# Seven unread 16-byte-row loads on the scalar engine's DMA queue, ahead of the first softmax of a decode block

## The chip, the cores and the metric

The kernel runs on one NeuronCore of a Trainium2 chip. The metric is the time of one execution on the device in microseconds (us); lower is better. The core has five engines with a queue of instructions each: PE (TensorE: matmuls, its weight loads shown as PEld), DVE (VectorE), ACT (ScalarE), POOL (GpSimd) and SP (SyncE, which here only issues DMAs). A transfer (a DMA) is issued by an instruction in the queue of SP or of ACT and is then carried by 16 DMA engines, which add to a semaphore as their shares land. In the trace SPq and ACTq are the issuing sides.

## What is computed

One decode step of a transformer block with adaptive layer norm, batch 2, one token each, all in float32: a modulation from a condition vector, attention of 32 query heads over the last 4096 positions of a cache with 8 key/value heads, and a feed-forward part.

```python
W = min(4096, max(256, Sk // 4))                      # 4096 of 32768 positions
q = (h @ wq) ...                                      # 32 heads of 128
k, v = k_cache[:, :, Sk - W:], v_cache[:, :, Sk - W:] # 8 heads, each for 4 query heads
p = softmax(q k^T * Dh ** -0.5);  attn = (p v) @ wo
mod = (silu(c) @ w_mod) -> sa, ca, ga, sb, cb, gb
x = x + ga * attn(layernorm(x) * (1 + ca) + sa)
x = x + gb * (silu((layernorm(x) * (1 + cb) + sb) @ w1) @ w2)
```

Nearly all the bytes are read once: 6.3 MB of `w_mod`, 8.4 MB of `wq`, 33.6 MB of keys, 33.6 MB of values, 8.4 MB of `wo`, 7.3 MB of `w1` and `w2`.

## The kernel before

All large inputs stream through one on-chip buffer, `slots` (line 68): a ring of eight slots of 16 KB on each of 128 partitions. `stream` (line 70) hands out slots in turn, and `load_runs` (line 88) and `load_pair` (line 77) issue one large DMA each on SP. In the order of SP's queue they are `w_mod` (three slots), the small `x`, `wq` (four slots), and then keys and values in pairs of slots. One step is one batch entry with two key/value heads; there are `STEPS` = 8 of them. The DMA of the keys of step s is called k0 to k7 here, that of the values v0 to v7, 4 MB each; each wants two free slots. `fetch` (line 349) issues them in the order k0, k1, v0, k2, v1, k3, v2, k4, and so on; `wo`, `w1` and `w2` follow (lines 506, 511, 600).

v0 and k2 go into the four slots that held `wq`, so they may start when the matmuls that make q (line 302) have read those slots. v1 goes into the slots of k0, k3 into those of k1, v2 into those of v0, and so on: a key load waits until DVE has transposed the keys that stood there (`keys`, line 361), and a value load until PE has used the old contents (`weighted`, line 448).

The work of a step: DVE transposes the keys (line 361), PE makes the scores (`scores`, line 374), DVE and PE find the maxima (`maxima`), ACT takes the exponential (`exponentials`: a copy of the bias at line 404, the activation at line 406), DVE and PE turn the weights (`turn`), ACT copies them to `ptb` (line 435), and PE multiplies them with the values (`weighted`, line 448). `place(0)` (line 334) comes ahead of step 0: it lays q out in `qbd` with copies on DVE, POOL and ACT (lines 319 and 329). `inorder` keeps an engine's instructions in the order in which they are written.

The framework gives each DMA one of eight semaphores (DMAHW0 to DMAHW7) to report its landing on. They are given out in turn, in the order in which the program's DMAs stand, over both issuing queues. A DMA that takes a semaphore which an earlier DMA has used waits for that earlier DMA to land before it is issued; the waits stand in the issuing engine's queue, which goes on with nothing behind them until they are met. In the program before, `w_mod` has DMAHW0, the four loads of `c` on ACT have 1 to 4, `x` has 5, `wq` 6, k0 7, k1 0 again, v0 1 again, k2 2, v1 3 and k3 4.

Of the kernel before, what the change touches and what calls it, by code (L numbers as in the profile page):

```python
# [13 lines left out]
P = 128  # L14
# [9 lines left out]
def adaln_block(  # L24
# [19 lines left out]
    nc = tc.nc  # L44
# [16 lines left out]
    def const(shape, name):  # L61
        return consts.tile(shape, F32, name=name)

    def bank(tag, name):
        return (psum1 if tag in "CO" else psum).tile([P, 512], F32, tag=tag, name=name)
# [244 lines left out]
    inorder = tc.keep_in_program_order  # L310

    def place(n):

        qT = once.tile([P, D], F32, tag="wide", name=f"qT{n}").rearrange("p (s j r) -> p s j r", s=4, r=32)
        inorder(nc.vector.transpose(qT.rearrange("p s j r -> p (s j r)"), q_ps[n]))  # L315
        for g in range(G):
            r = slice(32 * g, 32 * g + 32)
            eng = nc.gpsimd if g % 2 else nc.vector
            inorder(eng.tensor_copy(  # L319
                qg[n][r, :, :, :, g], qT[r, :, :, 0:32:16].rearrange("p s j b -> p s b j")  # L320
            ))
        rp = bank("C", f"qr{n}")[:, :P]
        inorder(nc.tensor.matmul(  # L323
            rp, rep4, qg[n].rearrange("p s b j g -> p (s b j g)"), start=True, stop=True
        ))
        for i in range(4):
            r = slice(32 * i, 32 * i + 32)
            cp = nc.scalar.copy if i % 2 else nc.vector.tensor_copy
            inorder(cp(
                qbd[n][r].rearrange("p s b j c -> p (s b j) c")[:, :, 4 * i : 4 * i + 4],  # L330
                rp[r, :].rearrange("p (m g) -> p m g", g=G),
            ))

    place(0)

# [394 lines left out]
```

## Time and profile before

| | |
|---|---|
| time, median of 2 runs | 235.64 us (235.56 to 235.73) |
| span of the profiled execution, first to last instruction | 233.7 us |
| own time of the profiled execution | not recorded beside its span; the timed runs lie 1.9 to 2.0 us above the span |
| bytes read | 97.53 MB, 417 GB/s over the span |
| PE busy | 161.1 us (69%) |
| DVE busy | 115.6 us (49%) |
| ACT busy | 28.5 us (12%) |
| POOL busy | 10.5 us (4%) |

The page of the profile gives busy time by engine, the DMA queues (q1 carries what SP issues, q10 what ACT issues, q8 and q14 instructions), and the chain of work that ended last. The timeline lists instructions with their start and length. The view of DMA issues tells how long after the start of its issue a DMA had fully landed. The view by windows gives for any stretch the mean busy share of the 16 DMA engines and the rate; shares a little above 1 come from counting each packet whole in the stretch in which it starts.

### The profile page before, as it was taken

The page shows a single profiled execution, that of the slowest core. Times are in us where ns is not written, and L with a number is a line of the kernel's source. Part 1 is how long each engine was busy: PE and PEld are TensorE (multiplying, and loading weights), DVE is VectorE, ACT ScalarE, POOL GpSimd, SP SyncE. Part 2 cuts the span into 40 slices and gives each one's busy share as a digit, 9 for nine tenths or more (in the row PEclk, how much of TensorE's full clock was granted, in tenths as well). Part 3 has the DMA queues.
Part 4 walks back from the last instruction along what each step waited for, and adds up shares of the span by engine and source line. Part 5 has one row for each costly group of instructions (what it writes and reads, how often), then busy time and mean ns, then how long its engine had stood idle before and what let it go on. Part 6 is the DMA issues. An engine that isn't in the chain of part 4 may idle for free.

```text
span 233.7 us, 2571 instructions
## 1 busy us (share of the span) xinstructions
PE 161.1 (69%) x1070; PEld 43.3 (19%) x1070; DVE 115.6 (49%) x179; ACT 28.5 (12%) x64; POOL 10.5 (4%) x35
## 2 busy tenths in 40 slices
PE   0004916859577839797598749759759779789684
PEld 0001401201111111211120201202112122324222
DVE  0007240278894758695197089259559540101232
ACT  2000210000311120120210201111020120102020
POOL 2004710000000000000000000000000000000000
PEclk9999985979999977999979999988997997999999
DMA  7998998999999999999999999999999999989991
GB/s 269 446 542 359 404 494 359 446 444 421 415 421 449 446 437 415 426 426 446 449 437 409 418 437 449 449 421 412 426 444 449 443 421 437 463 367 437 424 404 57
DMA packets 3794, 97.68 MB, mean 418 GB/s; under 512 B 432, under 2 KB 456, under 8 KB 968
## 3 DMA queue, kind: packets, MB, share of 16 engines
q1 hardware_dynamic: 3768, 97.53, 97.1%
q8 instruction: 8, 0.13, 0.2%
q14 instruction: 2, 0.02, 0.0%
q10 hardware_dynamic: 16, 0.00, 0.0%
HBM read 97.53 MB, written 0.00 MB: 417 GB/s over the span
## 4 chain that ended last, share of the span: by engine, by line
DMA 60%; issue 18%; DVE 14%; PE 6%; POOL 0%; SPq 0%; POOLq 0%; ACT 0%
DMA slots<-in_A_k_cache_dram 22%; DMA slots<-in_A_wq_dram 15%; DMA slots<-in_A_v_cache_dram 12%; DMA slots<-in_B_w_dram 12%; DVE kT L361 11%; PE o L448 2%; PE q L302 2%; DVE zp L420 1%; PE acc_yw L661 1%; DVE xp L418 1%; PE qr L323 0%; PE acc_y L671 0%; DVE qT L315 0%; POOL qg L319 0%; SPq L109 0%
## 5 line engine op out<-in xcount | busy, mean ns | idle before, releaser
L361 DVE STREAM_TRANSPOSE kT<-slots 128x1024 f32<-128x1024 f32 x64 | 73.7, 1212 | 23.7 <-DMA slots<-in_A_k_cache_dram 23.6
L374 PE MATMUL s<-kT,qbd 128*32 128x512 f32 x256 | 68.6, 693 | 19.1 <-DVE kT L361 18.0
L448 PE MATMUL o<-slots,ptb 128*32 128x512 f32 x256 | 30.8, 624 | 2.1 <-DMA slots<-in_A_v_cache_dram 2.1
L374 PEld LDWEIGHTS s<-kT,qbd 128*32 128x32 f32 x256 | 9.6, 113 | 68.4 <-DVE kT L361 63.4
L269 PE MATMUL m_a<-slots,scT 128*32 128x256 f32 x32 | 4.4, 506 | 20.5 <-DVE scT L261 20.5
L302 PE MATMUL q<-slots,hq_T 128*32 128x512 f32 x64 | 8.3, 680 | 7.0 <-DMA slots<-in_A_wq_dram 7.0
L448 PEld LDWEIGHTS o<-slots,ptb 128*32 128x32 f32 x256 | 8.1, 114 | 17.9 <-issue 17.8
L404 ACT COPY bias<-bp 128x1 f32<-128x1 f32 x8 | 1.3, 159 | 77.0 <-PE bp L402 77.0
L384 DVE TENSOR_REDUCE mx<-s 128x1 f32<-128x512 f32 x8 | 5.5, 691 | 9.6 <-PE s L374 9.6
L565 PE MATMUL junk<-quad,id 128*32 128x512 f32 x22 | 10.2, 595 | 0.0
L420 DVE TENSOR_TENSOR zp<-xp,quarter 128x1024 f32<-128x1024 f32 x8 | 9.8, 1225 | 0.2
L435 ACT ACTIVATE ptb<-pT,odd 128x256 f32<-128x256 f32 x16 | 6.7, 472 | 25.6 <-PE pT L427 25.6
L255 DVE STREAM_TRANSPOSE cT<-xc 128x128 f32<-128x128 f32 x1 | 0.4, 401 | 16.7 <-DMA xc<-in_c_dram 16.7
L427 PE MATMUL pT<-zp,mix 128*32 128x256 f32 x64 | 5.7, 428 | 3.6 <-DVE zp L420 3.5
L458 ACT COPY ob<-o 128x512 f32<-128x512 f32 x8 | 4.7, 585 | 26.1 <-PE o L448 26.1
L272 PE MATMUL m_sp<-slots,scT 128*32 128x512 f32 x32 | 7.4, 738 | 0.0
L386 PE MATMUL mT<-ident,mx 128*1 128x128 f32 x16 | 3.0, 270 | 6.3 <-DVE mx L384 6.3
L315 DVE STREAM_TRANSPOSE qT<-q 128x512 f32<-128x512 f32 x2 | 1.4, 717 | 11.7 <-PE q L302 10.2
L418 DVE STREAM_TRANSPOSE xp<-pr 128x512 f32<-128x512 f32 x8 | 5.5, 686 | 3.4 <-ACT pr L406 3.4
L579 PE MATMUL acc_o<-slots,oTn 128*32 128x512 f32 x56 | 6.2, 593 | 0.7 <-DMA slots<-in_A_wo_dram 0.7
L466 PE MATMUL o_all<-ob,selh 128*64 128x128 f32 x64 | 6.0, 316 | 0.8 <-ACT ob L458 0.8
L550 DVE COPY acc_o_sb<-acc_o 128x256 f32<-128x256 f32 x1 | 0.4, 425 | 12.4 <-ACT acc_o_sb L549 12.4
(140 smaller groups left out, 93.8 us busy)
## 6 DMA issues: line engine op xcount, KB each, us to landing
slots<-in_A_k_cache_dram SPq DMA_DIRECT2D x8, 4096.0 KB, 27.4
slots<-in_A_v_cache_dram SPq DMA_DIRECT2D x8, 4096.0 KB, 27.6
slots<-in_w_mod_dram SPq DMA_DIRECT2D x1, 6144.0 KB, 17.1
slots<-in_A_wo_dram SPq DMA_DIRECT2D x1, 6144.0 KB
slots<-in_B_w_dram SPq DMA_DIRECT2D x1, 2688.0 KB
slots<-in_A_wo_dram SPq DMA_DIRECT2D x1, 2048.0 KB, 29.5
slots<-in_B_w_dram SPq DMA_DIRECT2D x1, 2048.0 KB
slots<-in_B_w_dram SPq DMA_DIRECT2D x1, 896.0 KB
```

The source lines that it names most:

```text
L272: nc.tensor.matmul(m_sp[r, :], scT[:, k, :], cd[:, g], start=(k == 0), stop=(k == 3))
L302: nc.tensor.matmul(q_ps[n][32 * g : 32 * g + 32, :], hq_T[:, k, :], wv[:, n, g], start=(k == 0), stop=(k == 3),)
L361: inorder(nc.vector.transpose(kT[s, j][:, 32 * c : 32 * c + 32, :], kt[s].rearrange("p (n j r) -> p j n r", j=4, r=32)[:, j, 32 * c : 32 * ...
L374: inorder(nc.tensor.matmul(s_ps[s][r : r + 32, :], qbd[h // 4][:, h % 4, b, j, :], kT[s, j][:, 32 * c : 32 * c + 32, e:32:2], start=(j == ...
L418: inorder(nc.vector.transpose(xp, pr[s]))
L420: inorder(nc.vector.tensor_mul(zp, xp[:, None, :, 0:16].to_broadcast([P, 4, 16, 16]), quarter[:, :, None, None].to_broadcast([P, 4, 16, 16 ...
L427: inorder(nc.tensor.matmul(tp[32 * i : 32 * i + 32, :], mix.rearrange("p v e -> p (v e)"), zp.rearrange("p y t x -> p (y t) x")[:, :, 4 * ...
L435: inorder(nc.scalar.activation(ptb[s % 2][:, :, e, :], tp.rearrange("p (w z) -> p w z", z=16), AF.Copy, scale=odd[:, e : e + 1],))
L448: inorder(nc.tensor.matmul(o_ps[s][r : r + 32, :], ptb[s % 2][:, w].rearrange("p e z -> p (e z)"), vt[s].rearrange("p (c w m f d) -> p c f ...
L466: inorder(nc.tensor.matmul(o_all[r : r + 64, :], selh[:, m, lo : lo + 2 * HQ], o_sb[s][:, m * DH : (m + 1) * DH], start=(s == 0 and m < 2) ...
L565: inorder(nc.tensor.matmul(junk[0:32, :], id4, quad.rearrange("p m y -> p (m y)"), start=True, stop=True,))
L579: inorder(nc.tensor.matmul(acc[32 * g : 32 * g + 32, :], oTn[:, q, :], wot[q], start=(q < 4), stop=(q >= 24),))
```

## The change

Three lines after `place(0)`: a small tile `spare`, and seven loads on ACT's queue of the first four elements (16 bytes) of the first 8, 12, 6, 14, 10, 1 and 3 rows of `w2`. Nothing reads `spare`. The output is computed as before.

```diff
     place(0)
+    spare = const([P, 7, 4], "spare")
+    for i, n in enumerate((8, 12, 6, 14, 10, 1, 3)):
+        inorder(nc.scalar.dma_start(spare[:n, i, :], w2[:n, :4]))
```

ACT's queue in the changed program, from the copy of the modulation through the copies of `place(0)` to the exponential of step 0; `spare` is the new tile, `in_B_w_dram` the input `w2`, and the names in brackets are the semaphores an instruction waits for (DMAHW: landings of DMAs, the others: engines):

```order
L286 COPY mod_sp<-m_sp 128x512 [waits PE_49]
L329 COPY qbd_151<-qr_280 32x32x4 [waits DVE_49] x2
L337 DMA spare<-in_B_w_dram 8x4 [waits DMAHW1_49]
L337 DMA spare<-in_B_w_dram 12x4 [waits DMAHW2_49]
L337 DMA spare<-in_B_w_dram 6x4 [waits DMAHW3_49]
L337 DMA spare<-in_B_w_dram 14x4 [waits DMAHW4_49]
L337 DMA spare<-in_B_w_dram 10x4 [waits DMAHW5_49]
L337 DMA spare<-in_B_w_dram 1x4 [waits DMAHW6_49]
L337 DMA spare<-in_B_w_dram 3x4 [waits DMAHW7_49]
L407 COPY bias_336<-bp_334 128x1 [waits PE_49]
L409 ACT_TABLE_LOAD [waits DVE_49]
```

Before, the bias copy (then line 404) followed directly on the copies of line 329. The seven loads stand between them and take the semaphores DMAHW1 to DMAHW7, each waiting for the landing of the DMA that had it: the four loads of `c`, `x`, `wq` and k0.

SP's queue before, the first six loads of keys and values (k0, k1, v0, k2, v1, k3):

```order
L82 DMA slots<-in_A_k_cache_dram 128x1x8192 [waits DMAHW0_49,PE_49]
L82 DMA slots<-in_A_k_cache_dram 128x1x8192 [waits PE_49]
L82 DMA slots<-in_A_v_cache_dram 128x1x8192 [waits DMAHW6_49,DMAHW1_49,PE_49]
L82 DMA slots<-in_A_k_cache_dram 128x1x8192 [waits DMAHW2_49,PE_49]
L82 DMA slots<-in_A_v_cache_dram 128x1x8192 [waits DMAHW7_49,DMAHW3_49,DVE_49]
L82 DMA slots<-in_A_k_cache_dram 128x1x8192 [waits DMAHW4_49,DMAHW0_49,DVE_49]
```

SP's queue in the changed program, the same six loads:

```order
L82 DMA slots<-in_A_k_cache_dram 128x1x8192 [waits DMAHW0_49,PE_49]
L82 DMA slots<-in_A_k_cache_dram 128x1x8192 [waits PE_49]
L82 DMA slots<-in_A_v_cache_dram 128x1x8192 [waits DMAHW6_49,DMAHW0_49,PE_49]
L82 DMA slots<-in_A_k_cache_dram 128x1x8192 [waits DMAHW1_49,PE_49]
L82 DMA slots<-in_A_v_cache_dram 128x1x8192 [waits DMAHW7_49,DMAHW2_49,DVE_49]
L82 DMA slots<-in_A_k_cache_dram 128x1x8192 [waits DMAHW3_49,DVE_49]
```

The loads stand in the same order. The seven new DMAs have moved the turn of the semaphores on: v0 now takes DMAHW0, which k1 has, and waits for it in place of DMAHW1, which a load of `c` had. k2, v1 and k3 wait for the semaphores of the first three new loads in place of those of the loads of `c`, and the wait of k3 for DMAHW0 (k1, whose slots it takes) is no longer there, since SP has met it already for v0. On PE, DVE and POOL the same instructions stand in the same order, with the semaphores of the loads renumbered.

## The prediction

> **What bounds the kernel now.** I read the page first, for the share of the DMA queues and the chain that ended last; then the view by windows, to see whether the DMA engines ever pause; then the timeline of SP and the view of DMA issues, for when each load is issued and lands; and last ACT and DVE at the place of the change. The page:
>
> ```profile
> span 233.7 us, 2571 instructions
> ...
> q1 hardware_dynamic: 3768, 97.53, 97.1%
> q8 instruction: 8, 0.13, 0.2%
> ...
> DMA 60%; issue 18%; DVE 14%; PE 6%; POOL 0%; SPq 0%; POOLq 0%; ACT 0%
> ```
>
> The queue of the large loads alone keeps 16 engines busy for 97.1% of the span, and DMA is the largest part of the last chain. By windows (the last two columns are the busy share of the DMA engines and GB/s):
>
> ```profile
> 0.00:1.70 1.70, 0.00 (x0) 0.00 (x0) 0.27 (x1) 0.00 (x0) 1.09 (x8) 1.00 0.00 0
> 1.70:4.20 2.50, 0.00 (x0) 0.00 (x0) 0.00 (x0) 0.38 (x1) 0.52 (x2) 1.00 0.98 315
> 36.00:56.00 20.00, 15.11 (x90) 3.69 (x90) 9.43 (x12) 0.51 (x2) 0.47 (x2) 0.82 1.01 434
> 56.00:76.00 20.00, 14.36 (x70) 2.80 (x72) 14.53 (x18) 4.00 (x9) 0.00 (x0) 1.00 0.99 429
> ...
> 176.00:196.00 20.00, 16.39 (x110) 4.93 (x112) 10.51 (x15) 2.26 (x6) 0.00 (x0) 0.85 1.00 429
> 196.00:216.00 20.00, 17.78 (x149) 6.60 (x140) 1.66 (x6) 2.24 (x3) 0.00 (x0) 0.98 0.99 424
> 216.00:226.00 10.00, 7.82 (x45) 2.31 (x44) 3.39 (x17) 1.77 (x3) 0.00 (x0) 1.00 0.98 419
> ```
>
> From 1.7 us on the DMA engines do not pause, up to 226. The chain of waits, three pieces of it:
>
> ```profile
> 92.88 22.90 DMA slots<-in_A_k_cache_dram
> ...
> 126.84 27.70 DMA slots<-in_A_k_cache_dram
> ...
> 165.61 27.61 DMA slots<-in_A_v_cache_dram
> ...
> 198.74 27.57 DMA slots<-in_B_w_dram
> 226.30 0.14 issue
> 226.44 1.92 PE acc_yw L661 x16
> ```
>
> k4 lands at 92.88 + 22.90 = 115.78, k6 at 154.54, v7 at 193.22. From k4 to k6 four loads land (v3, k5, v4, k6), from k6 to v7 four more: 38.76 / 4 and 38.68 / 4, so a load of 4096 KB takes 9.68 us, or 433 GB/s, at both places. The end hangs on the same stream: the first large piece of `w2` lands at 226.30 and PE starts on it at once. So the kernel is one unbroken stream of bytes, and 233.7 - 226.3 = 7.4 us of the span are left when that piece is in. There is no later pause in which a delay of the stream could be made good: a pause of the DMA engines in the middle comes out at the end, one for one.
>
> **The seven loads themselves.** Where they stand:
>
> ```profile
> 46.40 0.26 ACT L329 COPY qbd<-qr 32x128 f32<-32x128 f32 x1 [15.43 <-DVE qbd L329]
> 47.01 0.26 ACT L329 COPY qbd<-qr 32x128 f32<-32x128 f32 x1 [0.35 <-DVE qbd L329]
> 60.61 0.16 ACT L404 COPY bias<-bp 128x1 f32<-128x1 f32 x1 [13.35 <-PE bp L402]
> ```
>
> The only loads on ACT before are the four of `c`:
>
> ```profile
> 1.16 2.62 ACTq L105 DMA_DIRECT2D xc<-in_c_dram  x4
> ```
>
> Issuing is 2.62 / 4 = 0.65 us each, so seven take 4.6 us: from 47.27 to 51.9, inside the 13.35 us in which ACT waits for PE. Their own semaphore waits cost nothing there: the last is for k0, which lands one load ahead of k1, and k1 lands at 57.8 (below), so at 48.1. Their 54 rows of 16 bytes are 864 bytes. Packets cost time too, and the nearest row is that of the packets of `c`, which pass beside `w_mod`, in the view of DMA queues from 6 to 17.3 us (packets, MB, share of 16 engines):
>
> ```profile
> q10 hardware_dynamic: 16, 0.00, 0.2%
> ```
>
> 0.2% of 16 engines for 11.3 us is 0.36 us for 16 packets, 0.02 us each. The first engine of the 16 gets at most seven rows and seven semaphore packets, some 0.3 us if all fall on one engine's bulk work. I take 0.1 and keep 0 to 0.4.
>
> **The wait that they move.** This is where I put the cost. In the changed order v0 waits for DMAHW0, held by k1 (the built program asks for a count of 32, 16 for `w_mod` and 16 for k1). When was v0 issued, and when does k1 land?
>
> ```profile
> 0.73 0.38 SPq L93 DMA_DIRECT2D slots<-in_w_mod_dram  x1
> ...
> 29.08 1.84 SPq L82 DMA_DIRECT2D slots<-in_A_k_cache_dram  x2
> 43.97 0.54 SPq L82 DMA_DIRECT2D slots<-in_A_v_cache_dram  x1
> 45.69 0.54 SPq L82 DMA_DIRECT2D slots<-in_A_k_cache_dram  x1
> 57.38 0.53 SPq L82 DMA_DIRECT2D slots<-in_A_v_cache_dram  x1
> ```
>
> The second of the two issues at 29.08, k1, starts at 30.37, and the view of DMA issues for that stretch says:
>
> ```profile
> slots<-in_A_k_cache_dram SPq DMA_DIRECT2D x1, 4096.0 KB, 27.4
> ```
>
> So k1 lands at 30.37 + 27.4 = 57.8. v0 goes from 43.97 to 57.8, and behind it on SP stand k2 (45.69, now 58.4) and v1 (57.38, now about 59). Before, two loads were queued when k1 ended; now none is: the stream runs dry once. k2 also waits for the first new load and v1 for the second. The four of `c` took until DVE could start on them, after 16.7 us of idle time:
>
> ```profile
> L255 DVE STREAM_TRANSPOSE cT<-xc 128x128 f32<-128x128 f32 x1 | 0.4, 401 | 16.7 <-DMA xc<-in_c_dram 16.7
> ```
>
> That is about 4 us each, one after the other, beside the bulk; issued from 47.3 on, the first two land by 52 and 56, before 58. The later ones are wanted by loads that are issued after 70.
>
> What does starting the stream again cost? The nearest row is the one start from nothing, `w_mod`:
>
> ```profile
> slots<-in_w_mod_dram SPq DMA_DIRECT2D x1, 6144.0 KB, 17.1
> ```
>
> At 433 GB/s its 6144 KB take 1.5 x 9.68 = 14.5 us, so the start costs 17.1 - 14.5 = 2.6 us from issue to landing. Issuing a key or value load takes 0.54 in place of 0.38, 0.16 more: 2.7. The Trainium skill, on "SBUF — State Buffer", section "The DMA setup-cost knee", gives every DMA a roughly fixed 2 us beside its bytes; by that the forecast below would be 238.1 in place of 238.8, and this trace's row says 2.6. As bounds: the windows show an empty 0.73 to 1.7, 1.0 us, as the least; the most I keep is 4.0, since a start in mid-program isn't shown.
>
> Who is late, then: v0 lands at 57.8 + 2.7 + 9.7 = 70.2, and PE wants it at 74.86, when the maxima of step 1 are done. k2 lands at 79.9 where DVE took it at 77.15:
>
> ```profile
> 74.86 3.64 PE L448 MATMUL o<-slots,ptb 128*32 128x512 f32 x32
> ...
> 77.15 2.37 DVE L361 STREAM_TRANSPOSE kT<-slots 128x1024 f32<-128x1024 f32 x2 [2.71 <-DMA slots<-in_A_k_cache_dram]
> ```
>
> DVE was waiting for it already, so from here on every step is 2.7 us late, and the stream with it.
>
> One more term. The 16 engines don't end a load together, and the trace tells a landing by the last. q8 fetches code: 8 packets, 0.2% of 16 x 233.7 us, so 0.9 us each, on one engine at a time. In an unbroken stream an engine that is ahead hides such a fetch; after the dry spell all 16 start level, and the next fetch shows at the end, in part or whole: 0 to 0.9, I take 0.4.
>
> The sum: 0.1 + 2.7 + 0.4 = 3.2 us on a span of 233.7, so 236.9; the median of the runs lies 1.94 above the span, so 238.8 us, or 1.4% more than 235.64.
>
> **The rivals.**
> *Nothing happens* (the wait is met in time, or the stream has a reserve). For it: v0 isn't wanted before 74.86. Against it: the DMA share, which has no hole to give back. It gives 235.6 to 236.1. The Trainium skill, on "DMA: Bandwidth & Descriptors", section "Issuing engines are not separate DMA queues", has DMAs from several engines interleave on the same 16 DMA engines, so that only the time to issue differs; by it alone this rival would hold, as it says nothing of a moved wait. The packets of q10 between those of q1 agree with it. 8%.
> *Slower by over 2%: a dearer restart.* The same dry spell with a price that `w_mod` at an idle chip doesn't show, or with code fetches falling on one engine after the engines have been levelled. It decides from 4.72 - 0.5 = 4.2 us on, against 2.7; two fetches on one engine (1.8 in place of 0.4) and a restart of 3 would reach it. It gives 240.4 to 242. For it: the price rests on one row. Against it: nothing in that row looks short. 10%.
> *The softmax is held up.* If ACT's queue were held until all seven had landed, that would be till about 47.3 + 7 x 4 = 75 and not 51.9, and the exponential of step 0 would come 14 us late; v1 and k3 would still be queued behind k2 till 57.8 + 2.7 + 3 x 9.7 = 89.6, so most of it is hidden and the result is that of the forecast or the rival above. It has no chance of its own.
> *Faster.* The uneven row counts delay low engines more than high ones; if that made them pass each other better, the rate would rise. To come out 2% faster, the stream left at 57.8, 226.3 - 57.8 = 168.5 us of it, would have to run 2.8% above the 433 GB/s that both stretches of the chain show, and there is no idle time of the DMA engines after 1.7 us to save. 2%, 230.9 at that point.
>
> **How the numbers follow.** The forecast has 80%, the null rival 8%, the dear restart 10%, faster 2%. The forecast's own range comes from the bounds: 1.0 to 4.0 for the restart, 0 to 0.4 for the packets, 0 to 0.9 for the levelling, which all at their ends would be 236.6 to 240.9; that all lie at one end is unlikely, so I take 237.0 to 240.3, which leaves out the null rival, the dear one and little more. Two per cent, 4.7 us, is about what a measurement of this kernel tells from no change: faster 0.02, within 0.88, slower 0.10.
>
> **What would show it.** SP should issue v0 at about 57.8 with a wait on a DMA, k2 and v1 within 1.5 us behind it, and the windows from 57 to 61 should show DMA shares far below 1, the only ones before the tail. k2's keys should start on DVE near 79.9, and every later load should land 2.7 to 3.6 us later than before. ACT's bias copy should stay at 60.6. If v0 is issued at 44, the step of the moved wait is wrong; if the dry spell is there and the end is not late, the claim that no reserve is left is wrong; if the stream is dry a second time, I have missed a wait.

## The result, and the profile after

The changed kernel takes 239.7 us (239.5 to 239.9, 2 runs) against 235.64: the ratio is 1.0169, with a 95% interval of 1.0139 to 1.0198, so 4.1 us more. The forecast was 238.8 us in a range of 237.0 to 240.3. The profiled execution spans 238.1 us, 4.4 more than before.

From the page after (span, DMA share in 40 slices of 6 us, queues):

```profile
span 238.1 us, 2578 instructions
...
DMA  7998989993999999999999999999999999999991
...
q1 hardware_dynamic: 3768, 97.53, 95.7%
...
q10 hardware_dynamic: 124, 0.01, 0.0%
```

The row of nines has one hole: the tenth slice, 53.6 to 59.5 us, has 3. The bytes are the same, and q10 has 108 packets more: 54 rows and 54 reports to a semaphore. The timeline of SP for the first value and key loads after k1 (start, length):

```profile
58.30 0.54 SPq L82 DMA_DIRECT2D slots<-in_A_v_cache_dram  x1
58.94 0.55 SPq L82 DMA_DIRECT2D slots<-in_A_k_cache_dram  x1
59.59 0.54 SPq L82 DMA_DIRECT2D slots<-in_A_v_cache_dram  x1
72.12 0.54 SPq L82 DMA_DIRECT2D slots<-in_A_k_cache_dram  x1
```

v0, k2 and v1 go out together behind k1's landing, where before they went at 43.97, 45.69 and 57.38. The view of waits on SP between 25 and 75 us names the releaser (total, times, longest):

```profile
SPq L82 <- DMA slots<-in_A_k_cache_dram: 27.8, 1, 27.8
```

The view by windows, the last two columns being DMA share and GB/s:

```profile
57.00:58.00 1.00, 0.96 (x6) 0.14 (x4) 0.80 (x1) 0.00 (x0) 0.00 (x0) 1.00 0.00 0
58.00:59.00 1.00, 0.94 (x4) 0.00 (x0) 0.01 (x1) 0.00 (x0) 0.00 (x0) 1.00 0.00 0
59.00:60.00 1.00, 0.26 (x2) 0.09 (x2) 0.69 (x1) 0.00 (x0) 0.00 (x0) 1.00 1.20 360
60.00:61.00 1.00, 0.48 (x4) 0.29 (x2) 0.81 (x3) 0.00 (x0) 0.00 (x0) 1.00 0.44 164
```

Packets are counted where they start, so the zeros mean that no packet of a large load starts in 57 to 59. In the trace's records of packets the last one of k1 ends at 57.83 and the first one of v0 starts at 59.66: the stream is dry in between. The view of DMA issues for v0, and DVE's wait for k2 in the timeline:

```profile
slots<-in_A_v_cache_dram SPq DMA_DIRECT2D x1, 4096.0 KB, 12.3
```

```profile
81.72 2.37 DVE L364 STREAM_TRANSPOSE kT<-slots 128x1024 f32<-128x1024 f32 x2 [6.84 <-DMA slots<-in_A_k_cache_dram]
```

v0 lands at 58.3 + 12.3 = 70.6; k2 lands 11.1 us after it and not 9.7, and DVE takes it at 81.72, 4.57 later than before. From there on the shift stays. The chain of waits at the end:

```profile
170.21 27.62 DMA slots<-in_A_v_cache_dram
...
203.34 27.21 DMA slots<-in_B_w_dram
230.55 0.14 issue
```

v7 lands at 197.83 (before 193.22, so 4.6 later), the first large piece of `w2` at 230.55 (226.30, 4.25 later). The seven loads themselves pass unseen on ACT: they are issued in 2.38 us, 0.34 each. The bias copy comes at 61.05, 0.44 later than before, which is what k0's landing was late by in this execution (48.57 against 48.13), before any packet of the small loads.

```profile
48.24 2.38 ACTq L337 DMA_DIRECT2D spare<-in_B_w_dram  x7
61.05 0.16 ACT L407 COPY bias<-bp 128x1 f32<-128x1 f32 x1 [12.56 <-PE bp L405]
```

### The profile page after: what moved, and what is told of

Read it like the earlier page. It is cut to its first block, busy times and chain, and to the rows that moved or that the text cites. A ratio compares the mean times of both kernels' runs of the same rounds, so it can differ in the third digit from the quotient of the medians.

```text
span 238.1 us, 2578 instructions
## 1 busy us (share of the span) xinstructions
PE 165.2 (69%) x1070; PEld 43.5 (18%) x1070; DVE 115.6 (49%) x179; ACT 28.5 (12%) x64; POOL 10.6 (4%) x35
## 4 chain that ended last, share of the span: by engine, by line
DMA 59%; issue 19%; DVE 13%; PE 7%; SPq 0%; POOL 0%; POOLq 0%; ACT 0%; DVEq 0%
DMA slots<-in_A_k_cache_dram 21%; DMA slots<-in_A_wq_dram 15%; DMA slots<-in_A_v_cache_dram 12%; DMA slots<-in_B_w_dram 11%; DVE kT L364 11%; PE q L302 3%; PE o L451 2%; DVE zp L423 1%; PE acc_yw L664 1%; DVE xp L421 1%; PE acc_y L674 0%; SPq L109 0%; POOL qg L319 0%; DVE qT L315 0%; PE acc_l L689 0%
## 5 line engine op out<-in xcount | busy, mean ns | idle before, releaser
L377 PE MATMUL s<-kT,qbd 128*32 128x512 f32 x256 | 71.0, 709 | 21.9 <-DVE kT L364 20.9
L302 PE MATMUL q<-slots,hq_T 128*32 128x512 f32 x64 | 9.4, 750 | 7.7 <-DMA slots<-in_A_wq_dram 7.7
L568 PE MATMUL junk<-quad,id 128*32 128x512 f32 x22 | 11.4, 655 | 0.0
L430 PE MATMUL pT<-zp,mix 128*32 128x256 f32 x64 | 6.2, 464 | 2.0 <-DVE zp L423 1.9
L582 PE MATMUL acc_o<-slots,oTn 128*32 128x512 f32 x56 | 7.0, 593 | 0.0
L272 PE MATMUL m_sp<-slots,scT 128*32 128x512 f32 x32 | 6.8, 718 | 0.0
L469 PE MATMUL o_all<-ob,selh 128*64 128x128 f32 x64 | 5.5, 294 | 0.8 <-ACT ob L461 0.8
```

Of the source, the lines that this page charges most:

```text
L272: nc.tensor.matmul(m_sp[r, :], scT[:, k, :], cd[:, g], start=(k == 0), stop=(k == 3))
L302: nc.tensor.matmul(q_ps[n][32 * g : 32 * g + 32, :], hq_T[:, k, :], wv[:, n, g], start=(k == 0), stop=(k == 3),)
L377: inorder(nc.tensor.matmul(s_ps[s][r : r + 32, :], qbd[h // 4][:, h % 4, b, j, :], kT[s, j][:, 32 * c : 32 * c + 32, e:32:2], start=(j == ...
L430: inorder(nc.tensor.matmul(tp[32 * i : 32 * i + 32, :], mix.rearrange("p v e -> p (v e)"), zp.rearrange("p y t x -> p (y t) x")[:, :, 4 * ...
L568: inorder(nc.tensor.matmul(junk[0:32, :], id4, quad.rearrange("p m y -> p (m y)"), start=True, stop=True,))
L582: inorder(nc.tensor.matmul(acc[32 * g : 32 * g + 32, :], oTn[:, q, :], wot[q], start=(q < 4), stop=(q >= 24),))
```

## The experiments

Two theories stood against each other: the moved wait of v0 lets the stream run dry, or the small packets disturb the DMA engines. Times are medians; each ratio is to runs of the kernel before on the same chip (235.45 to 235.53 us).

### Other numbers of loads

**Eight loads.**

```diff
-    spare = const([P, 7, 4], "spare")
-    for i, n in enumerate((8, 12, 6, 14, 10, 1, 3)):
+    spare = const([P, 8, 4], "spare")
+    for i, n in enumerate((8, 12, 6, 14, 10, 1, 3, 8)):
```

> Theory (the moved wait): an eighth load takes DMAHW0 in v0's place, so v0 takes DMAHW1 and waits for the first new load, which landed near 55 in the changed kernel. v0 is then queued some 2 us before k1 ends, the stream does not run dry, and the time is 235.6 to 236.3 us. Rival (the small packets disturb the 16 DMA engines): more small packets than in the changed kernel, so 239.7 us or more.

Measured: 236.49 us, ratio 1.0039 (1.0028 to 1.0050). Three quarters of the loss are gone with one load more. The 0.9 us that are left lie above the theory's range. The windows and the issues on SP show where they begin:

```profile
55.00:56.00 1.00, 0.97 (x8) 0.14 (x4) 1.00 (x2) 0.00 (x0) 0.00 (x0) 1.00 0.34 132
56.00:57.00 1.00, 0.97 (x6) 0.14 (x4) 1.00 (x2) 0.00 (x0) 0.00 (x0) 1.00 1.59 492
57.00:58.00 1.00, 0.97 (x6) 0.14 (x4) 0.69 (x1) 0.00 (x0) 0.00 (x0) 1.00 0.46 197
58.00:59.00 1.00, 0.84 (x4) 0.00 (x0) 0.12 (x1) 0.00 (x0) 0.00 (x0) 1.00 0.92 393
```

```profile
54.87 0.54 SPq L82 DMA_DIRECT2D slots<-in_A_v_cache_dram  x1
57.12 0.54 SPq L82 DMA_DIRECT2D slots<-in_A_k_cache_dram  x1
```

v0 now waits for the first new load and goes out at 54.87, 3.0 us ahead of k1's landing at 57.88; its first packet starts at 56.19. From 55.8 to 56.7 only 4 to 13 of the 16 engines have a packet in the trace: those ahead wait for v0's first bytes. The stream stumbles but doesn't stop; how that comes to 0.9 us is told behind the table below.

**Six loads** (the last row count left out of the list).

> Theory: with six loads v0 takes DMAHW7 and waits for k0, which lands at 48, so it is issued at 48; now k2 waits for k1 (57.8), but v0 is in flight then. No dry spell: 235.6 to 236.1 us. Rival (small packets): six sevenths of the extra time, about 239.1 us.

Measured: 235.69 us, ratio 1.0001 (0.9991 to 1.0011).

```profile
48.39 0.54 SPq L82 DMA_DIRECT2D slots<-in_A_v_cache_dram  x1
58.06 0.53 SPq L82 DMA_DIRECT2D slots<-in_A_k_cache_dram  x1
```

v0 goes at k0's landing, and it is now k2 that goes at k1's landing, with v0 in flight. The same late issue of a large load costs nothing while another one is queued well ahead.

**Fifteen loads** (the list of seven, 8, and the list of seven again).

> Fifteen loads turn the semaphores once more: v0 waits for the eighth new load, which itself is issued by ACT only when k1 has landed (57.8 to 58.4). Theory: the dry spell grows by one small load from issue to landing, 1.5 to 2.5 us beside idle DMA engines, v0 issued at 59.8 to 60.9, and the time is 241.2 to 242.4 us. Rival (small packets): twice the extra time of the changed kernel, 243.5 us or more. If the spell doesn't grow: 239.7 us.

Measured: 240.62 us, ratio 1.0224 (1.0206 to 1.0241), 0.9 us above the changed kernel. The waits on SP between 25 and 75 us and v0's issue:

```profile
SPq L82 <- DMA spare<-in_B_w_dram: 28.6, 1, 28.6
```

```profile
59.12 0.54 SPq L82 DMA_DIRECT2D slots<-in_A_v_cache_dram  x1
```

v0 is issued 0.8 us later than in the changed kernel and not 1.5 to 2.5. Measured from k1's landing, which came at 57.81 here and at 58.25 there, the spell grows by 1.3 us: the eighth small load lands at 59.07, 1.26 behind k1, so a small load beside idle DMA engines is quicker than I put it. Twice the packets do not make twice the loss.

### The loads without the wait, and the wait without the loads

**Seven loads of one row.** The row counts are all 1.

> Seven loads of one row each, the semaphores as in the changed kernel. Theory: the same wait and the same dry spell, 239.2 to 240.0 us, v0 issued near 58.3. Rival (small packets, uneven row counts): a third of the packets or fewer and no graded delay of the engines, so 236 to 237 us.

Measured: 239.72 us, ratio 1.0178 (1.0162 to 1.0193), v0 issued at 58.00. With 7 rows in place of 54 the loss is the same, so neither the amount of traffic nor the uneven row counts make it.

**Seven loads on POOL's queue.**

```diff
-        inorder(nc.scalar.dma_start(spare[:n, i, :], w2[:n, :4]))
+        inorder(nc.gpsimd.dma_start(spare[:n, i, :], w2[:n, :4]))
```

> The same seven loads issued by POOL; they take no DMAHW semaphore, and v0 waits as in the kernel before. Theory: v0 is issued near 44 and the time is 235.6 to 236.3 us. Rival (small packets): the same rows pass the same DMA engines, 239 us or more.

Measured: 236.33 us, ratio 1.0032 (1.0019 to 1.0045). The page has the same rows on another queue, with more packets than on ACT's (224 against 108), and SP issues v0 as early as the q matmuls let it:

```profile
q0 software_dynamic: 224, 0.00, 0.1%
```

```profile
45.63 0.53 SPq L82 DMA_DIRECT2D slots<-in_A_v_cache_dram  x1
```

The large loss is gone. Of the 0.8 us left, 0.2 are in the span (233.9) and the rest lies outside it; what that is was not followed up.

**The wait alone.** No small load is left. POOL, idle there, copies one element from k1's slots into v0's ahead of v0's load, and the loads are kept in their order on SP.

```diff
         t = stream(2)
+        if after is not None:
+            inorder(nc.gpsimd.tensor_copy(t[0:1, 0:1], after[0:1, 0:1]))
-        nc.sync.dma_start(
+        inorder(nc.sync.dma_start(
...
-            vt[s - 1] = load_pair(v_cache, s - 1)
+            vt[s - 1] = load_pair(v_cache, s - 1, kt[s] if s - 1 in (0,) else None)
```

> None of the seven loads: POOL copies one element of k1's tile into v0's tile ahead of v0's load, so that v0 waits for k1. Theory: the dry spell alone makes the whole loss, 239.3 to 240.0 us, v0 issued near 58.3. Rival (small packets): nothing is left of the loss, 235.6 to 235.9 us.

Measured: 239.67 us, ratio 1.0172 (1.0155 to 1.0189): the whole loss. v0 goes at 58.12; the windows from 57 to 59 are empty again:

```profile
57.00:58.00 1.00, 0.97 (x6) 0.14 (x4) 0.39 (x1) 0.00 (x0) 0.08 (x1) 1.00 0.00 0
58.00:59.00 1.00, 0.54 (x4) 0.00 (x0) 0.41 (x1) 0.00 (x0) 0.10 (x1) 1.00 0.00 0
```

**The same wait, k2 ahead of v0.** The same copy, without `inorder` around the loads; k2 then stands ahead of v0 on SP.

> The same wait of v0 for k1, but k2 stands ahead of v0 in SP's queue and does not wait. Theory: k2 is in flight when k1 ends, the stream does not run dry, 235.6 to 236.3 us. Rival (a late v0 costs by itself, since its values come late to PE): 238 us or more, as v0 then lands near 77 where PE wanted it at 74.9.

Measured: 235.59 us, ratio 1.0007 (0.9997 to 1.0016).

```profile
45.86 0.53 SPq L84 DMA_DIRECT2D slots<-in_A_k_cache_dram  x1
58.10 1.18 SPq L84 DMA_DIRECT2D slots<-in_A_v_cache_dram  x2
```

k2 goes at 45.86 and lands at 67.44, where v0 landed before. v0 still goes at 58.1, with v1 behind it, lands at 77.10, and costs nothing, because k2 keeps the engines busy. It is the hole in the stream that costs, not the late values.

### What one dry spell costs

**A dry spell at v3** (the same copy, from k4's slots to v3's).

> One dry spell in another place: v3 waits for k4, which lands near 115.8 in the kernel before. Theory (no reserve anywhere): restart 2.5 to 3.2 us plus the lead that the engines lose, 0 to 1.4: 238.2 to 240.2 us. Rival (the place matters, since softmax and place(1) of the first steps stood in the way at v0): under 237 us.

Measured: 240.19 us, ratio 1.0195 (1.0180 to 1.0211). v3 goes at 116.20 behind k4, and the windows are empty there too:

```profile
115.00:116.00 1.00, 0.00 (x0) 0.00 (x0) 0.12 (x1) 0.01 (x1) 0.00 (x0) 1.00 0.00 0
116.00:117.00 1.00, 0.00 (x0) 0.00 (x0) 1.00 (x1) 0.00 (x0) 0.18 (x1) 0.79 0.00 0
```

There is no reserve at this place either. By the medians the spell costs 0.5 us more here than at v0; why was not followed up.

**Dry spells at v0 and v3.**

> Dry spells at v0 and at v3. Theory with the lost lead paid at each dry spell: twice the loss of one, 8.1 us, 243.0 to 244.2 us. Variant in which a code fetch shows once and only the restart of 2.5 to 3.0 us is paid twice: 241.9 to 242.8 us. Rival (a reserve in the middle takes it up): 239.7 us.

Measured: 244.27 us, ratio 1.0368 (1.0353 to 1.0384), 8.7 us: about the sum of the two alone (4.1 and 4.7).

**Dry spells at v0 and at k2**, right after one another: v0 waits for k1, k2 for v0.

> Two dry spells with no code fetch between them: v0 waits for k1 (about 57.8) and k2 waits for v0 (about 70.5), while the next fetch comes near 78.7 us in every run so far. Theory (each spell costs a restart of 3.0 to 3.1 us, and the first fetch after the last spell 1.1 to 1.4 us once): 3.0 + 2.9 + 1.3, so 242.4 to 243.0 us. Rival (each spell costs 4.1 to 4.6 us whatever lies between, as at v0 and v3 together): 243.8 to 244.6 us.

Measured: 242.96 us, ratio 1.0320 (1.0304 to 1.0337), 7.5 us. The windows of both spells:

```profile
57.00:58.00 1.00, 0.97 (x6) 0.14 (x4) 0.40 (x1) 0.00 (x0) 0.07 (x1) 1.00 0.00 0
58.00:59.00 1.00, 0.54 (x4) 0.00 (x0) 0.41 (x1) 0.00 (x0) 0.11 (x1) 1.00 0.00 0
59.00:60.00 1.00, 0.38 (x2) 0.09 (x2) 0.49 (x2) 0.00 (x0) 0.00 (x0) 1.00 1.56 459
70.00:71.00 1.00, 0.97 (x6) 0.14 (x4) 1.00 (x2) 0.00 (x0) 0.17 (x1) 1.00 0.00 0
71.00:72.00 1.00, 0.97 (x6) 0.14 (x4) 0.69 (x1) 0.00 (x0) 0.00 (x0) 1.00 0.00 0
72.00:73.00 1.00, 0.84 (x4) 0.00 (x0) 0.11 (x1) 0.00 (x0) 0.00 (x0) 1.00 1.68 524
```

Two spells cost 1.2 us less here than at v0 and v3, though the dry windows look alike. What differs is what lies between them. The trace has the time at which each of the 16 engines reports its share of a load; here are, for some loads, the first, the last but one and the last report (us), with the last one's shift against before:

| load | before | changed | at v0 and v3 | at v0 and k2 |
|---|---|---|---|---|
| v0 | 65.65, 67.05, 67.46 | 70.13, 70.53, 70.62 (+3.2) | 70.03, 70.50, 70.56 (+3.1) | 70.07, 70.44, 70.50 (+3.0) |
| k2 | 75.33, 76.71, 77.12 | 79.80, 80.27, 81.70 (+4.6) | 79.70, 80.20, 81.71 (+4.6) | 82.69, 83.17, 84.46 (+7.3) |
| k4 | 114.05, 115.77, 115.78 | 118.76, 120.38, 120.43 (+4.7) | 118.42, 120.35, 120.37 (+4.6) | 121.59, 123.08, 123.13 (+7.4) |
| v3 | 123.73, 125.45, 125.50 | 128.43, 130.03, 130.08 (+4.6) | 132.53, 133.08, 133.09 (+7.6) | 131.27, 132.73, 132.85 (+7.4) |
| k5 | 133.41, 135.18, 135.37 | 138.09, 139.75, 139.97 (+4.6) | 142.25, 142.81, 144.24 (+8.9) | 140.95, 142.51, 142.75 (+7.4) |

Before, the engines are spread over 1.8 us from v0 on. Behind a dry spell all 16 start level: the spread of v0 is 0.5, and the shift 3.0 to 3.2. (In the changed kernel 0.45 of the 3.2 was there at k1, and 0.44 at k0 already; in the runs with POOL's copy 0.3 lies between k1's landing and v0's issue.) Then one engine falls behind by 1.3 to 1.4 us within one load (k2 in the changed kernel; k5 behind the spell at v3), and the load's landing is that engine's. The queue view of the changed kernel from 77 to 83 us has what happens there:

```profile
q1 hardware_dynamic: 95, 2.59, 100.5%
q8 instruction: 1, 0.02, 1.0%
```

One code fetch: 1.0% of 16 engines for 6 us is 0.96 us, and the packet of the large load behind it on the same engine takes 1.68 us in the trace where the others take 1.21: together 1.4. The kernel before has a fetch at the same place (78.90), but on an engine that was ahead, and its landings don't move. Between v0 and v3 two fetches come (78.64 and 108.83), so that the second spell makes the engines that are ahead wait for the late ones again and the next fetch is paid anew; between v0 and k2 there is none (the next comes at 78.97), and 3.0 + 3.0 + 1.3 make up the 7.3 of the table.

Eight loads show the lost lead by itself, without a restart. There v0 and k2 land only 0.1 later than before (67.56 and 77.21), but v0's first report comes at 66.72 in place of 65.65: the engines that were ahead lost 1.1 us of their lead at the stumble. The next fetch, at 78.80, falls into v1, which lands at 87.91 in place of 86.80, with one engine 1.0 behind the other 15. That is the 0.9 us. The part of the fetches is read from the traces; no run moves or removes a fetch.

## Why the prediction was right, step by step

*The moved wait: right.* v0 was issued at 58.30, k2 and v1 within 1.3 us behind it; forecast were 57.8, 58.4 and about 59. The wait alone makes the whole loss, and the loads without that wait make little or none of it.

*No reserve: right.* The shift of 4.6 at k2 stays to v7, and 4.25 are left at the first piece of `w2`; a spell at v3 costs no less, two cost about the sum. The rival in which nothing happens fell with the first profile.

*The restart: right.* 2.7 us were put down from the start of `w_mod`; 12.3 - 9.7 = 2.6 came out. The 2 us of the Trainium skill ("SBUF — State Buffer", "The DMA setup-cost knee") are too little here, as the row of `w_mod` already said. The rival of a dearer restart fell; what it also named, a fetch that costs more once the engines are levelled, is the last term below.

*The seven loads on ACT: right.* 2.38 us of issuing, put down as 4.6, both inside the wait for PE. The first two landed at 55.15 and 57.31, not by 52 and 56, but still ahead of v0's issue. Their packets were taken at 0.1 us on the stream, and it was less: from k0's landing to k1's it is 9.68 us in the changed kernel, 9.68 with one row each, 9.71 with fifteen loads, and 9.67 before. k1 did land 0.45 later than before in the changed kernel, but k0 had been late by 0.44 in that execution, and its late engine was behind before any small load had a packet.

*The levelled engines: the term that was mis-sized.* "0 to 0.9, I take 0.4": it was 1.4 at k2, and 1.1 of that are left at the end. The mechanism was that of the prediction. What was off is the price of a code fetch, 0.9 us by the share of its own packets, where the bulk packet behind it loses another 0.5; and that fetches keep coming, 17 to 37 us apart in both traces, so that the first one after a spell is paid in full and not in half. The 0.3 that go missing by the end are lost by the kernel before: its 16 reports spread over 1.71 us at v7 and over 2.05 at the first large piece of `w2`, the changed kernel's over 1.59 and 1.56. With nothing for the packets, 2.7 for restart and wake-up, and 1.1 in place of 0.4, the sum is 3.8 us against a forecast of 3.2; the 0.45 by which this execution was late at k0 make it 4.25, the shift at the first piece of `w2`. In the run of the wait alone, where k1 is on time, the parts are 2.9 and 1.3, together 4.2.

Two of the signs named ahead came out too small for the same reasons: DVE took k2 at 81.72 and not near 79.9, and the later loads landed 4.6 later and not 2.7 to 3.6. The levelling alone went beyond its bound of 0.9; that the time still lies in the range is owed to the room left for the restart, up to 4.0, and is luck as far as this term goes.

*The rivals of the softmax and of a faster stream:* ACT's bias copy came at 61.05 against 60.61, late by no more than k0 was, so the softmax wasn't held up. A stream fast enough to gain 4.7 us would have needed a rate 2.9% higher rather than 2.8. Uneven row counts neither cost nor gain anything, by the run with one row each.

Fifteen loads and eight loads fell outside what the theory expected of them, by 0.6 below and 0.2 above, and POOL's queue and the two spells at v0 and v3 by less than 0.1; fifteen loads are the same wait in another size, and eight loads are the levelled engines without a dry spell. No kernel tried beats the one before, whose stream already has no hole.

## What to carry to other kernels

Where DMAs share a small set of semaphores in turn, an extra DMA, however small, changes for which earlier DMA each later one waits; look at the waits of the large loads behind it, not at its bytes. In a kernel that lives on one unbroken stream of loads, what counts is whether the next load is there when the first DMA engine is done with its share of the one in flight, and not the last: a late issue well under cover is free (six loads), one that comes when the engines ahead run out costs their lead at the next code fetch (eight loads, 0.9 us), and a hole costs the restart plus that lead (seven loads, 4.1 us). If such a DMA is needed, its number is the remedy to try first: six or eight in place of seven gave back all or three quarters of the loss.

## What was not expected of the hardware

A fetch of code delays one DMA engine by 1.4 us, though its packet takes 0.96: the packet of 32 KB after it took 1.68 in place of 1.21 us. In an unbroken stream this shows about once: after the late engine of k0 (46.28, 46.88 and 48.13 for the first, the last but one and the last report, before) five more fetches pass until v7, at 193 us, and the landings keep their distance of 9.7 us.

A small load beside the bulk is slow in turns, not in bytes. In the changed kernel the first packets of the seven loads start at 52.1, 3.9 us after the first issue, and an engine's row and its report each wait for a bulk packet of 1.21 us. The Trainium skill ("DMA: Bandwidth & Descriptors", "Queues, rings and completion order") has each engine take turns between its queues by packet, which agrees; here such a packet of the bulk queue is a whole row of 32 KB.
